# Cached grouped-query attention: the first key load cut into four transfers of interleaved partitions

## The chip, the core and the metric

The kernel runs on one core of a Trainium2 chip. The time is device time in microseconds (us) of one execution; the kernel before was timed three times. A separate execution under the hardware profiler gives the profile and the trace. The engines are named as the profile names them: PE (matrix multiply; PEld is its weight load), DVE (vector), ACT (scalar), POOL, and SP, which here only issues transfers. Transfers are carried by 16 DMA engines that work in parallel; SP and ACT each have a queue of their own that feeds them (q1 and q10 in the profile).

## The reference

Four query positions for each of 8 batches attend to a cache of 2048 keys; four query heads share one key/value head. All arrays are bf16.

```
B, Sq, D = 8, 4, 512
Hq, Hkv, Sk, Dh = 32, 8, 2048, 128
q = (x @ wq).reshape(B, Sq, Hq, Dh), heads ahead of positions
k = jnp.repeat(k_cache, rep, axis=1)
v = jnp.repeat(v_cache, rep, axis=1)
scores = jnp.einsum("bhqd,bhkd->bhqk", q, k) * (Dh ** -0.5)
p = _softmax(scores, axis=-1)
o = jnp.einsum("bhqk,bhkd->bhqd", p, v)
out = o, positions ahead of heads, reshaped (B, Sq, Hq * Dh) @ wo
```

The K cache and the V cache are 33.55 MB each, wq and wo 4.19 MB each, x and the output 32 KB each. All of it is read or written once, 75.56 MB.

## The kernel before

The work is cut into 8 passes (`NU`), numbered u = 0 to 7. A pass takes 8 pairs of a batch and a key/value head: 4 heads of batches 6 and 7 in pass 0, all 8 heads of one batch in passes 1 to 6 (`single(u)`), the other 4 heads of batches 6 and 7 in pass 7. A pass needs one K tile and one V tile of 4.19 MB each, 128 partitions by 32 KB. In passes 0 and 7 a tile has two members, one for each of the two batches, of 16 KB in a partition; a V tile has two members in every pass.

The tiles go through `ring`, a buffer with four slots (`NR`). The list `loads` fixes their order: K0, wq, K1, V0, K2, V1, K3, V2, K4, V3, K5, V4, K6, V5, K7, V6, V7, wo. `issue(done)` sends out every load whose slot is free by then: four loads ahead of the first pass, and two more after each later pass. Transfers are issued by SP, in this order, and SP waits until the slot's last reader has finished. The one exception is the second member of K0, which ACT issues, so that both members start together.

`load_kv` issues one tile. With `by_member` it makes two transfers, one for each member (line 133: 128 partitions by 16 KB, 2 MB each); with `whole` one transfer of 4 MB; with `by_half` two that each hold one half of both members. The list `split` names the loads that go by member: V0, V1, V2, V3 and K7; K0 does so by its own call. The last V goes by halves, all others go whole. wo is loaded in six pieces that get smaller to the end (line 146): 2 MB, 1 MB, 512 KB, 256 KB, 128 KB, 128 KB. Each transfer of 128 partitions has eight partitions for each of the 16 DMA engines.

Completion is told by eight counters that the transfers take in turn. A transfer waits until the one that had its counter before, eight transfers earlier, has landed.

A pass does this: DVE transposes K in eight steps (`turn(u, i, t)`, line 213; t is a quarter of the tile, and i in passes 0 and 7 is the member), in the order t = 0 with i = 0 and 1, t = 1 with i = 0 and 1, and so on. PE multiplies each turned quarter with the queries (`scores`, line 251, 32 matmuls in a pass). DVE takes the maximum (line 264), ACT the exponential (line 291), DVE transposes the weights (line 305), and copies spread them into `p_bd` (line 315). Then PE multiplies the weights of the pass before with its V tile (`values(u - 1, h)`, line 331, two halves of 32 matmuls; the right side of each matmul holds both members of V). PE's order in a pass is `scores(u)`, then the collecting of an earlier pass's output by tokens (`by_tokens`, line 375), then `values(u - 1)`. After pass 7 come `values(7, 0)`, `by_tokens(6)`, `values(7, 1)`, `project(0, 0, 4)`, `by_tokens(7)`, `project(0, 4, 16)` and `project(1, 0, 16)`. `project(gg, r0, r1)` multiplies with wo row block by row block (line 403, two matmuls for each r); r = 0 to 15 of gg = 1 are the ones that need the five small pieces of wo, cut at r = 8, 12, 14 and 15.

Ahead of pass 0, x goes through PE (line 416) and is multiplied with wq (line 425).

Of the kernel before, what the change touches and what calls it, by code (L numbers as in the profile page):

```python
# [17 lines left out]
def kernel(  # L18
# [9 lines left out]
    nc = tc.nc  # L28
# [8 lines left out]
    G = 4  # L37
    S = 128 // G
    C = Sk // S
    NG = Hkv // G  # L40
    NB = 2
    NU = B * Hkv // (G * NB)
    NS1 = NU - NG
    FIRST, LAST = 0, NU - 1
# [28 lines left out]
    ring = ring_pool.tile([128, NR, NB, C * Dh], BF16, name="ring")  # L73
# [14 lines left out]
    def single(u):  # L88
        return FIRST < u < LAST

    def half_of(u):
        return NG - 1 if u == LAST else 0
# [8 lines left out]
    def take(key):  # L101
        slot_of[key] = n_loads[0] % NR
        n_loads[0] += 1
        return slot_of[key]
# [2 lines left out]
    by_half = [(0, 0.5), (0.5, 1)]  # L107
    by_member = None

    def load_kv(kind, u, parts, engines=(nc.sync,)):  # L110

        slot = take((kind, u))
        cache = k_cache if kind == "k" else v_cache
        n = C * Dh
        if not single(u):
            rows = cache[NS1:, G * half_of(u) : G * half_of(u) + G].rearrange(
                "b g (s c) d -> (g s) b (c d)", c=C
            )
        elif kind == "v":
            rows = cache[u - 1].rearrange("(b g) (s c) d -> (g s) b (c d)", g=G, c=C)  # L120
        else:
            rows = cache[u - 1].rearrange("h (s c) d -> (h s) (c d)", c=NS * C)
        if kind == "k" and single(u):
            pairs = [(ring[:, slot, :, :].rearrange("p b n -> p (b n)"), rows)]
        elif parts is by_member:
            pairs = [(ring[:, slot, b, :], rows[:, b]) for b in range(NB)]
        else:
            pairs = [
                (ring[:, slot, :, int(h0 * n) : int(h1 * n)], rows[:, :, int(h0 * n) : int(h1 * n)])
                for h0, h1 in parts  # L130
            ]
        for i, (to, of) in enumerate(pairs):
            engines[i % len(engines)].dma_start(to, of)

    def load_wq():
        slot = take("wq")
        nc.sync.dma_start(
            ring[:, slot, :, :].rearrange("p b n -> p (b n)"), wq.rearrange("(p r) n -> p (r n)", r=R)
        )

    def load_wo():
        slot = take("wo")
        for gg, cuts in ((0, (0, RW)), (1, (0, 8, 12, 14, 15, RW))):
            rows = wo[gg * G * 512 : (gg + 1) * G * 512, :].rearrange("(p r) j -> p (r j)", r=RW)
            for r0, r1 in zip(cuts, cuts[1:]):
                nc.sync.dma_start(ring[:, slot, gg, r0 * D : r1 * D], rows[:, r0 * D : r1 * D])  # L146
# [5 lines left out]
            loads.append(("k", u + 2))  # L152
    loads.append("wo")
    loads.reverse()
    split = [("v", 0), ("v", 1), ("v", 2), ("v", 3), ("k", NU - 1)]

    def issue(done):

        while loads and n_loads[0] < done + NR:
            what = loads.pop()  # L160
            if what == "k0":
                load_kv("k", 0, by_member, (nc.sync, nc.scalar))
                nc.sync.dma_start(x_sb[:, :], x.flatten_outer_dims())
            elif what == "wq":
                load_wq()
            elif what == "wo":
                load_wo()
            elif what in split:
                load_kv(*what, by_member)
            else:  # L170
                load_kv(*what, by_half if what == ("v", NU - 1) else whole)

    issue(0)

    make_identity(nc, ident[:])
# [266 lines left out]
    for u in range(NU + 1):  # L442
# [19 lines left out]
        if u >= 1:  # L462
# [7 lines left out]
            if u == NU:  # L470
                joined(u - 1)
        issue(2 + 2 * u)

    o_last = psum_o.tile([128, DH], FP32, tag="o", name="o_last")
# [40 lines left out]
```

## Time and profile before

| what | us |
|---|---|
| median of three runs (184.38 to 184.55) | 184.46 |
| the profiled execution: its own time | 184.68 |
| the profiled execution: its span | 182.7 |
| PE busy | 135.3 (74%) |
| DVE busy | 128.5 (70%) |
| ACT busy | 70.2 (38%) |
| POOL busy | 39.1 (21%) |
| time of the packets of q1 and q10, share of 16 DMA engines | 94.2% + 2.7% |

The span is the part of the profiled execution between its first and last recorded work; 1.98 us of its own time lie outside it. The busy times of several engines add to more than the span since they work side by side. 75.70 MB in 182.7 us are 414 GB/s over the whole span, with the empty stretches at its ends counted.

### The profile page before, as it was taken

Reading aid. Unit: us, or ns where it says so; the run is one execution under the profiler, and the core shown is the slowest. Engines: PE = TensorE matmul, PEld = TensorE weight load, DVE = VectorE, ACT = ScalarE, POOL = GpSimd, SP = SyncE. Lnnn points to the kernel's source line nnn. Section 1 sums busy time; section 2 is a strip of 40 time slices with the busy share of each in tenths; the row PEclk is TensorE's granted clock in tenths of the full one; section 3 lists DMA queues with packets and bytes.
Section 4 is the critical chain, followed back from the end, with each engine's and each line's share of the span. In section 5 each row is a group of like instructions: output and inputs, shape, how many; then the busy total and the mean of one; then the engine's idle time right before and its main releaser. Section 6 shows DMA issues by size and latency. Waiting matters only on the chain.

```text
span 182.7 us, 2386 instructions
## 1 busy us (share of the span) xinstructions
PE 135.3 (74%) x924; PEld 83.0 (45%) x924; DVE 128.5 (70%) x161; ACT 70.2 (38%) x91; POOL 39.1 (21%) x110
## 2 busy tenths in 40 slices
PE   0000077922999989998999995989399977899993
PEld 0000022400358536833963682358234852388971
DVE  6518024749985997899599856995399559967340
ACT  2000020049407912970692098009900792073010
POOL 8800006008003400700160052004400220023000
PEclk9999996996599999999999999999879999999999
DMA  6999999999999998999999999999999999999991
GB/s 226 430 484 402 416 459 405 430 445 441 459 384 430 447 459 382 430 441 459 395 427 438 459 407 427 434 452 452 387 434 423 434 427 434 414 429 436 427 367 40
DMA packets 5066, 75.70 MB, mean 414 GB/s; under 512 B 512, under 2 KB 832, under 8 KB 1088
## 3 DMA queue, kind: packets, MB, share of 16 engines
q1 hardware_dynamic: 4912, 73.47, 94.2%
q10 hardware_dynamic: 144, 2.10, 2.7%
q8 instruction: 7, 0.11, 0.2%
q14 instruction: 3, 0.02, 0.0%
HBM read 75.53 MB, written 0.03 MB: 414 GB/s over the span
## 4 chain that ended last, share of the span: by engine, by line
DMA 43%; DVE 27%; PE 17%; issue 5%; ACT 3%; POOL 2%; SPq 1%; ACTq 0%; DVEq 0%; POOLq 0%
DVE kt L213 18%; DMA ring<-in_k_cache_dram 16%; DMA ring<-in_wo_dram 16%; DMA ring<-in_wq_dram 12%; PE s_ps L251 11%; DVE stat L264 4%; PE o_ps L331 4%; ACT p_sb L291 3%; PE psq L425 2%; DVE pt L305 2%; DVE stat L322 1%; POOL p_bd L315 1%; POOL q_bd L231 1%; SPq L146 1%; DVE stat L272 0%
## 5 line engine op out<-in xcount | busy, mean ns | idle before, releaser
L213 DVE STREAM_TRANSPOSE kt<-ring 128x1024 f32<-128x1024 f32 x64 | 73.9, 1208 | 15.2 <-DMA ring<-in_k_cache_dram 12.8
L251 PE MATMUL s_ps<-kt,q_bd 128*128 128x512 bf16 x256 | 68.2, 403 | 21.7 <-POOL q_bd L231 9.9
L331 PE MATMUL o_ps<-ring,p_bd 128*128 128x256 bf16 x512 | 57.2, 273 | 0.0
L251 PEld LDWEIGHTS <-q_bd 128*128 128x128 bf16 x256 | 24.9, 101 | 63.5 <-issue 27.6
L331 PEld LDWEIGHTS <-p_bd 128*128 128x128 bf16 x512 | 49.8, 98 | 6.0
L315 ACT COPY p_bd<-pt 32x1024 bf16<-32x1024 bf16 x44 | 45.8, 1040 | 1.5 <-DVE pt L305 1.1
L291 ACT ACTIVATE p_sb<-s_ps,stat 128x1024 bf16<-128x1024 f32 x16 | 17.7, 1110 | 72.6 <-DVE stat L272 72.6
L315 POOL COPY p_bd<-pt 32x1024 bf16<-32x1024 bf16 x16 | 17.0, 1062 | 106.4 <-DVE pt L305 93.7
L264 DVE TENSOR_REDUCE stat<-s_ps 128x1 f32<-128x1024 f32 x16 | 19.2, 1203 | 2.9 <-PE s_ps L251 2.8
L305 DVE STREAM_TRANSPOSE pt<-p_sb 128x512 f32<-128x512 f32 x16 | 11.4, 711 | 14.0 <-ACT p_sb L291 14.0
L231 POOL COPY q_bd<-qT 32x64 bf16<-32x64 bf16 x64 | 13.0, 229 | 20.5 <-DVE qT L436 18.8
L425 PE MATMUL psq<-ring,xT_sb 128*32 128x512 bf16 x32 | 3.4, 604 | 9.1 <-DMA ring<-in_wq_dram 9.1
L416 PE MATMUL xtp<-ident,x_sb 32*128 32x32 bf16 x4 | 0.3, 194 | 13.3 <-DMA x_sb<-in_x_dram 13.3
L436 DVE STREAM_TRANSPOSE qT<-q_sb 128x64 f32<-128x64 f32 x8 | 1.2, 213 | 8.6 <-ACT q_sb L432 8.6
L177 DVE MEMSET p_bd<- 128x2048 uint32 x3 | 5.3, 1765 | 2.0 <-PEq L499 1.2
L322 DVE TENSOR_SCALAR stat<-of_b,stat 128x2 f32<-128x2 f32 x8 | 6.3, 791 | 0.3
L416 PEld LDWEIGHTS <-x_sb 32*128 32x128 bf16 x4 | 0.2, 114 | 13.3 <-DMA x_sb<-in_x_dram 13.3
L425 PEld LDWEIGHTS <-xT_sb 128*32 128x32 bf16 x32 | 1.3, 139 | 10.6 <-issue 10.1
L432 ACT CAST q_sb<-psq 128x512 bf16<-128x512 f32 x2 | 1.2, 586 | 11.7 <-PE psq L425 11.7
L375 PEld LDWEIGHTS <-perm 128*128 128x128 bf16 x56 | 3.8, 97 | 1.9 <-issue 0.4
L403 PE MATMUL s_ps<-ring,oP 128*32 128x256 bf16 x32 | 4.4, 272 | 0.2
L419 ACT COPY xT_sb<-xtp 128x128 bf16<-128x128 bf16 x1 | 0.3, 266 | 11.2 <-PE xtp L416 11.2
(30 smaller groups left out, 45.3 us busy)
## 6 DMA issues: line engine op xcount, KB each, us to landing
ring<-in_k_cache_dram SPq DMA_DIRECT2D x6, 4096.0 KB, 24.1
ring<-in_v_cache_dram SPq DMA_DIRECT2D x10, 2048.0 KB, 25.3
ring<-in_v_cache_dram SPq DMA_DIRECT2D x3, 4096.0 KB, 30.1
ring<-in_k_cache_dram SPq DMA_DIRECT2D x3, 2048.0 KB, 27.2
ring<-in_wq_dram SPq DMA_DIRECT2D x1, 4096.0 KB, 21.0
ring<-in_k_cache_dram ACTq DMA_DIRECT2D x1, 2048.0 KB, 12.3
ring<-in_wo_dram SPq DMA_DIRECT2D x1, 2048.0 KB, 25.8
ring<-in_wo_dram SPq DMA_DIRECT2D x1, 1024.0 KB, 27.8
```

The lines of the kernel that those rows point to most:

```text
L177: nc.vector.memset(t[:, :, :, :, :], 0.0)
L213: nc.vector.transpose(out=out, in_=in_)
L231: nc.gpsimd.tensor_copy(out=qb[k * 32 : (k + 1) * 32, m, :, g, b, :].rearrange("w (j e) q -> w j e q", e=2), in_=qT[of * 32 : (of + 1) * 3 ...
L251: nc.tensor.matmul(s_ps[t // 2][:, t % 2, :], lhsT=q_bd[u % 2][:, m, 2 * j + e, :, :, :].rearrange("w g b q -> w (g b q)"), rhs=rhs, start ...
L264: nc.vector.tensor_reduce(out=stats[u][0][:, h : h + 1], in_=s_ps[h][:, :, :].rearrange("q t n -> q (t n)"), axis=AX, op=ALU.max, negate=True,
L291: nc.scalar.activation(out=out, in_=in_, func=EXP, bias=stats[u][1][:, :], scale=scale, accum_out=stats[u][2][:, h : h + 1],)
L305: nc.vector.transpose(out=pt[:, :, :, :].rearrange("s c q e -> s (c q e)").bitcast(FP32), in_=ps[u, h][:, :, :, :].rearrange("q c s e -> q ...
L315: copy(out=pb[rows, :, g, :, :], in_=pt[rows, :, :, :])
L322: nc.vector.tensor_scalar_mul(stats[u][3][:, :], of_b[:, :], stats[u][4][:, :])
L331: nc.tensor.matmul(o_pss[u][:, :, :], lhsT=pbs[u, h][:, i // 2, :, :, i % 2].rearrange("s g q -> s (g q)"), rhs=v[:, :, key_of(u, h, i // ...
L403: nc.tensor.matmul(out_ps[half], lhsT=oP[gg][:, r, :], rhs=w[:, r, half * DH : (half + 1) * DH], start=(gg == 0 and r == 0), stop=(gg == N ...
L425: nc.tensor.matmul(psq[g * T : (g + 1) * T, :], lhsT=xT_sb[:, r, :], rhs=w[:, (g * NB + gg) * rep * Dh : (g * NB + gg + 1) * rep * Dh], st ...
```

## The change

A new function `load_first` issues K0. Its second member is still one transfer from ACT, issued beside the first piece. Its first member goes from SP in four transfers of interleaved partitions: 0, 8, 16 ... (16 partitions), 1, 3, 5 ... (64), 2, 6, 10 ... (32), and 4, 12, 20 ... (16). They are 256 KB, 1 MB, 512 KB and 256 KB; each partition's row of 16 KB stays one run. Each of the 16 groups of eight neighbouring partitions has 1, 4, 2 and 1 partitions in them.

Three loads that went by member now go whole: V2, V3 and K7. That is three transfers fewer, so the number of transfers in the kernel stays 32, and from V6 on each has the counter that it had.

```diff
-    def load_kv(kind, u, parts, engines=(nc.sync,)):
+    def load_first():
+
+        slot = take(("k", FIRST))
+        rows = k_cache[NS1:, :G].rearrange("b g (s c) d -> (g s) b (c d)", c=C)
+        for i, (p, step) in enumerate(((0, 8), (1, 2), (2, 4), (4, 8))):
+            nc.sync.dma_start(ring[p::step, slot, 0, :], rows[p::step, 0])
+            if i == 0:
+                nc.scalar.dma_start(ring[:, slot, 1, :], rows[:, 1])
+
+    def load_kv(kind, u, parts):
...
-        for i, (to, of) in enumerate(pairs):
-            engines[i % len(engines)].dma_start(to, of)
+        for to, of in pairs:
+            nc.sync.dma_start(to, of)
...
-    split = [("v", 0), ("v", 1), ("v", 2), ("v", 3), ("k", NU - 1)]
+    split = [("v", 0), ("v", 1)]
...
             if what == "k0":
-                load_kv("k", 0, by_member, (nc.sync, nc.scalar))
+                load_first()
                 nc.sync.dma_start(x_sb[:, :], x.flatten_outer_dims())
```

Nothing that is computed changes, and the order of the instructions on PE, DVE, ACT and POOL is the same.

## The prediction

> **What bounds the kernel now.** I read the page first. Its lines on the DMA engines decide the rest:
>
> ```profile
> span 182.7 us, 2386 instructions
> ...
> DMA  6999999999999998999999999999999999999991
> ...
> DMA 43%; DVE 27%; PE 17%; issue 5%; ACT 3%; POOL 2%; SPq 1%; ACTq 0%; DVEq 0%; POOLq 0%
> ```
>
> The DMA engines are busy from the first slice to the last, and no engine of the core comes near that (PE 74%). The chain names DVE and PE for some stretches only because a transfer is issued when they free its slot; the row of nines says that the queue holds work all the same. So the end is the start of the stream, plus bytes over rate, plus what follows the last piece of wo. Next I looked at the start in short windows (time of each engine, then granted clock, DMA share, GB/s; a packet of 16 KB is booked where it begins, which is why a share can exceed 1):
>
> ```profile
> 1.70:1.85 0.15, 0.00 (x0) 0.00 (x0) 0.15 (x1) 0.15 (x1) 0.15 (x1) 1.00 3.40 874
> 1.85:2.40 0.55, 0.00 (x0) 0.00 (x0) 0.55 (x1) 0.55 (x1) 0.55 (x2) 1.00 0.74 238
> 2.40:2.70 0.30, 0.00 (x0) 0.00 (x0) 0.30 (x1) 0.06 (x1) 0.30 (x1) 1.00 0.00 0
> 1.74:5.74 4.00, 0.00 (x0) 0.00 (x0) 3.25 (x3) 0.72 (x1) 4.00 (x3) 1.00 1.01 385
> 100.00:170.00 70.00, 60.26 (x423) 39.57 (x421) 53.33 (x66) 31.16 (x40) 12.68 (x30) 0.98 1.00 428
> 179.40:181.20 1.80, 0.51 (x4) 0.12 (x3) 0.41 (x1) 0.36 (x1) 0.00 (x0) 1.00 0.00 0
> 181.20:181.40 0.20, 0.00 (x0) 0.00 (x0) 0.00 (x0) 0.00 (x0) 0.00 (x0) 1.00 0.42 118
> ```
>
> 874 GB/s x 0.15 us = 131 KB, eight packets; 238 x 0.55 = 131 KB, eight more; then none until 2.70. So eight of the 16 engines begin by 1.85 and the other eight straggle in over the next half microsecond. Steadily, a packet takes 16 x 16.38 KB / 428 GB/s = 0.61 us. The first eight take 3.40 x 0.15 x 16 / 8 = 1.02 us each, the second eight 0.74 x 0.55 x 16 / 8 = 0.81. From 1.74 to 5.74 the stream is (428 - 385) x 4.00 / 428 = 0.40 us short; as booking at the start flatters a window by half a packet on average (0.30), the **start loss** is about 0.7 us. The last two rows are the output's transfer of 32 partitions, used below.
>
> SP's queue (start, duration) gives the price of an issue:
>
> ```profile
> 0.75 0.37 SPq L133 DMA_DIRECT2D ring<-in_k_cache_dram  x1
> 1.17 0.42 SPq L163 DMA_DIRECT2D x_sb<-in_x_dram  x1
> 1.64 0.42 SPq L137 DMA_DIRECT2D ring<-in_wq_dram  x1
> 34.41 0.33 SPq L133 DMA_DIRECT2D ring<-in_k_cache_dram  x1
> 180.42 0.35 SPq L484 DMA_DIRECT2D out_dram<-out_sb  x1
> ```
>
> Then passes 6 and 7, where the change touches K7 (start, duration, engine, count, idle before):
>
> ```profile
> 130.87 6.88 DVE L213 STREAM_TRANSPOSE kt<-ring 128x1024 f32<-128x1024 f32 x6 [3.21 <-DMA ring<-in_k_cache_dram]
> ...
> 141.62 7.15 PE L331 MATMUL o_ps<-ring,p_bd 128*128 128x256 bf16 x64
> ...
> 147.18 1.23 DVE L213 STREAM_TRANSPOSE kt<-ring 128x1024 f32<-128x1024 f32 x1
> ...
> 150.26 5.75 DVE L213 STREAM_TRANSPOSE kt<-ring 128x1024 f32<-128x1024 f32 x5 [1.85 <-DMA ring<-in_k_cache_dram]
> ...
> 160.04 10.64 PE L331 MATMUL o_ps<-ring,p_bd 128*128 128x256 bf16 x96
> ```
>
> and the last matmuls with wo:
>
> ```profile
> 177.91 0.27 PE L403 MATMUL s_ps<-ring,oP 128*32 128x256 bf16 x1
> ...
> 178.29 0.27 PE L403 MATMUL s_ps<-ring,oP 128*32 128x256 bf16 x1
> ...
> 179.00 0.27 PE L403 MATMUL s_ps<-ring,oP 128*32 128x256 bf16 x1
> ...
> 179.34 0.27 PE L403 MATMUL s_ps<-ring,oP 128*32 128x256 bf16 x1
> ...
> 179.64 0.27 PE L403 MATMUL s_ps<-ring,oP 128*32 128x256 bf16 x1
> ```
>
> In pass 7 the first turn (147.18) is done with K7's first member alone; DVE then idles 1.85 us for the second. In the tail PE paces itself at 0.108 us per row block until r = 7 (177.91), and from there waits for each piece of wo: r = 8 at 178.29, 12 at 179.00, 14 at 179.34, 15 at 179.64.
>
> **The change, part by part.** *The start.* The first piece has one packet for each of 16 engines. Whether all 16 then begin together no row shows for 16 partitions. The nearest is the output's transfer: issued at 180.42, its first packet begins between 181.25 and 181.30 (narrower windows), 0.83 to 0.88 us later, while the 128-partition K0 needed 0.95 to 1.00 (0.75 to 1.70-1.75). So the first packet moves forward by 0 (if 0.95 belongs to a cold queue) to 0.15 us. The straggling of the second eight, 0.03 to 0.66 us behind the first, some 0.4 on average, is worth about 0.2 averaged over 16 engines and up to 0.6 on the slowest. Against it: packets that begin together may all take the 1.02 us of the first eight, not 0.81: minus 0.1. What counts is the slowest engine, since a landing is complete with its last engine. Bounds for the gain g: -0.1 (nothing is gained, eight packets take 0.2 us more) and 0.85 (all of the 0.7 goes, and 0.15 of head start). I take **g = 0.35 us**: 0.6 for the slowest engine's late begin less 0.2 to 0.4 for its longer first packet, plus 0.05 of head start. Nothing starves behind the first piece: ACT's half gives every engine eight packets (4.9 us) and the second piece is issued at 0.75 + 0.42.
>
> *More issues on SP.* Three more, at the spacing of the rows above (0.42 and 0.47), put x's issue from 1.17 to about 2.5, wq's to 3.0, K1's to 3.4, V0's to 4. K0 alone keeps the DMA engines to 1.74 + 4.19 MB / 428 GB/s = 11.5, so each of them still enters a full queue: 0. x goes to PE ahead of wq, which waits until 22.71 for its data, so x may be 9 us late for nothing. The work of four transfers in place of one: r = 14 and r = 15 wait for pieces of 128 KB that come 179.64 - 179.34 = 0.30 us apart, and 131 KB / 428 GB/s is 0.31. A further transfer in a full queue costs the stream nothing that shows; bounds 0 and 3 x 0.03, taken 0.
>
> [...]
>
> *The counters.* SP's issue of V0's second half comes to wait for ACT's half of K0, which lands at about 13 us (the first turn begins at 12.94). Until then 14.7 MB have been issued and about 4.9 moved; the 9.8 MB left cover 23 us, and the next issue, K2 at 34.41, waits for DVE anyway: 0. Without that cover it would be 9 us.
>
> *V2 and V3 whole.* Each matmul of L331 reads both members, so a first member alone starts nothing: 0. *K7 whole* takes away the early turn. Now all eight turns follow the landing, as in pass 6: from its first turn to its values matmuls 141.62 - 130.87 = 10.75 us (pass 5: 111.25 to 122.00, the same 10.75). Pass 7 then starts its values at 150.26 - g + 10.75 = 161.01 - g in place of 160.04. PE runs almost without a pause from there to r = 7, so that stretch shifts by +0.97 - g: r = 7 at 178.88 - g. The pieces of wo land g earlier, and PE meets them later: without waits r = 15 follows eight steps of 0.108 later, at 179.75 - g, against 179.64 with waits now. Of 0.97 us, 0.86 are hidden by the waits for wo and **0.11 reach the end**. Bounds: 0 (if PE closes up elsewhere) and 0.97 (if the pieces of wo moved with it).
>
> **Sum**: +0.11 - 0.35 = -0.24 us. On the profiled execution's 184.68 us that makes 184.44; the median of the runs is 0.22 lower, so on its scale **184.2 us**, 0.13% below 184.46. Under about 0.2% (0.37 us) a measurement of this kernel can't be told from no change.
>
> **The rivals.**
> 1. *The start gain is large* (g of 0.6 to 0.85): the slowest engine loses straggle and long first packet both, or PE makes up its 0.11. For it: the output's transfer starts quickly. Against: the eight that did begin together were the ones with 1.02 us. Price: 0.11 - 0.7 = -0.6, 183.85 us.
> 2. *The split gains nothing* (g = 0): the stragglers come from the queue's own first use, and ACT's simultaneous half, not from 128 partitions in one transfer. Then K7's 0.11 stands alone: 184.57 us. [...]
> 3. *Slower: PE runs at half clock in pass 7's scores.* PE is idle from 148.8 until the first turn of K7 ends, 2.4 us in place of 1.9. The windows of granted clock show a half-speed stretch behind idle times of 2.6 us (26.1 to 28.7), 3.1 (129.2 to 132.3) and over 4 (40 to 44.6), none behind 2.2 (110.4 to 112.6); it decides from somewhere between. In pass 6 one such stretch of 3.4 us was made up. In pass 1 two followed each other, and its scores ended 1.8 us after the last turn in place of 1.1: 0.7 late, with no slack left in the tail. 184.46 + 0.11 + 0.7 - 0.35 = 184.9 us; with g near 0 it is 185.3.
>
> **Chances.** Forecast 0.47 (within it 0.05 fall below the bound), rival 1 0.33, rival 2 0.08, rival 3 0.12. That makes faster 0.38, same 0.42 + 0.08 = 0.50, slower 0.12. The forecast's own range, g from 0.1 to 0.6, is 183.95 to 184.5. For 8 in 10 I go to 183.7, the far half of rival 1 (g = 0.85, to 183.72), and to 184.8, short of rival 3.
>
> **What would show it.** Right: 16 packets beginning within 0.15 us at 1.6 to 1.75, the first window without a straggle; x issued at 2.5; eight turns of K7 in one run behind its landing near 149.9, values of pass 6 near 160.7, and the last row blocks of wo at an even 0.108 us with no waits. Wrong: a second group of engines starting late again (rival 2), a granted clock of 0.5 between 150 and 160 (rival 3), waits for wo still there at the end (K7's cover was not needed), or a thin slice in the DMA row near 13 to 35 us (the counter's wait was not covered).

## The result and the profile after

The changed kernel is slower. Six runs have a median of 187.16 us (186.55 to 188.04), six of the kernel before on the same chip 184.51 us (184.38 to 184.84): a ratio of 1.0146, with a 95% interval of 1.0115 to 1.0177. The profiled execution took 187.35 us with a span of 185.5, which is 2.8 us more span than before. Some executions of such kernels are disturbed and some per cent longer (189.2 to 191.4 us for the kernel before, beside the experiments); the ratios here leave them out, and since the profiles of three experiments (act_late, both_on_sp, by_columns) are of such executions, only their first 12 us are read.

The profile page after (span, the DMA row of 40 slices, shares of the chain of waits):

```profile
span 185.5 us, 2389 instructions
...
DMA  6999999999999999999999999999999999999990
...
DMA 41%; PE 27%; DVE 20%; issue 4%; ACT 3%; POOL 2%; SPq 2%; ACTq 0%; DVEq 0%; POOLq 0%
```

The row of nines is unbroken, so the DMA engines were never without work. That does not say how much they carried. The same windows of both kernels do (start and end, width, the five engines, granted clock, DMA share, GB/s). Before:

```profile
1.74:5.74 4.00, 0.00 (x0) 0.00 (x0) 3.25 (x3) 0.72 (x1) 4.00 (x3) 1.00 1.01 385
5.74:8.74 3.00, 0.00 (x0) 0.00 (x0) 1.75 (x3) 0.00 (x0) 2.51 (x10) 1.00 1.02 437
8.74:10.74 2.00, 0.00 (x0) 0.00 (x0) 0.00 (x0) 0.00 (x0) 0.00 (x0) 1.00 1.01 434
10.74:16.74 6.00, 0.31 (x4) 0.31 (x5) 3.80 (x4) 0.27 (x1) 0.00 (x0) 1.00 1.01 434
16.74:32.74 16.00, 7.39 (x43) 2.71 (x43) 5.05 (x12) 1.17 (x2) 3.24 (x16) 0.89 1.00 431
32.74:102.74 70.00, 60.19 (x355) 33.80 (x353) 59.58 (x70) 34.84 (x43) 15.55 (x46) 0.95 1.01 432
```

After:

```profile
1.74:5.74 4.00, 0.00 (x0) 0.00 (x0) 3.25 (x3) 0.69 (x1) 4.00 (x3) 1.00 0.99 336
5.74:8.74 3.00, 0.00 (x0) 0.00 (x0) 1.75 (x3) 0.00 (x0) 2.52 (x10) 1.00 1.02 284
8.74:10.74 2.00, 0.00 (x0) 0.00 (x0) 0.00 (x0) 0.00 (x0) 0.00 (x0) 1.00 0.98 418
10.74:16.74 6.00, 0.32 (x4) 0.21 (x4) 0.51 (x1) 0.04 (x1) 0.00 (x0) 1.00 1.07 374
16.74:32.74 16.00, 4.44 (x36) 1.84 (x37) 7.61 (x14) 1.39 (x3) 2.44 (x12) 0.98 0.99 428
32.74:102.74 70.00, 60.65 (x352) 33.81 (x350) 57.40 (x68) 34.85 (x43) 16.45 (x50) 0.93 1.01 432
```

The missing bytes of a window, divided by 431 GB/s, are time. The first window lost (385 - 336) x 4.00 / 431 = 0.45 us, the second 1.06, the third 0.07, the fourth 0.84, the fifth 0.11 and the sixth nothing: 2.5 us, nearly all of the loss, and all in the time in which K0 and what was queued beside it moved. At 1.02 the engines are as busy from 5.74 to 8.74 as before, but each packet lasts longer. The mean time of a packet is the share times 16 engines times 16.38 KB over the rate: 1.02 x 262 / 284 = **0.94 us**, where before it is 1.02 x 262 / 437 = **0.61 us**.

The packets of each queue from 0 to 5 us (packets, MB, share of the 16 engines) show the other thing. Before, and then after:

```profile
q1 hardware_dynamic: 43, 0.70, 39.6%
q10 hardware_dynamic: 32, 0.52, 26.4%
```

```profile
DMA packets 64, 1.05 MB, mean 210 GB/s; under 512 B 0, under 2 KB 0, under 8 KB 0
...
q10 hardware_dynamic: 64, 1.05, 65.2%
```

Before, the two halves of K0 run side by side from the start. After, SP's queue (q1) has no packet at all in the first 5 us. Yet SP issued its pieces from 0.74 on (its timeline: start, duration, count):

```profile
0.74 2.52 SPq L115 DMA_DIRECT2D ring<-in_k_cache_dram  x4
3.31 0.58 SPq L172 DMA_DIRECT2D x_sb<-in_x_dram  x1
3.93 0.42 SPq L146 DMA_DIRECT2D ring<-in_wq_dram  x1
...
11.41 0.80 SPq L142 DMA_DIRECT2D ring<-in_v_cache_dram  x2
```

In narrow windows SP's first packet begins at 5.42 us, when ACT's queue (q10) has begun 73 of its 128. The first piece of 256 KB lands 8.2 us after its issue, at 8.9 us.

Pass 7 and the end (start, duration; the values of pass 6 are the line with L340):

```profile
152.63 6.88 DVE L222 STREAM_TRANSPOSE kt<-ring 128x1024 f32<-128x1024 f32 x6 [2.99 <-DMA ring<-in_k_cache_dram]
...
163.39 7.80 PE L340 MATMUL o_ps<-ring,p_bd 128*128 128x256 bf16 x70
...
181.81 0.27 PE L412 MATMUL s_ps<-ring,oP 128*32 128x256 bf16 x1
...
181.91 0.27 PE L412 MATMUL s_ps<-ring,oP 128*32 128x256 bf16 x1
...
182.03 0.27 PE L412 MATMUL s_ps<-ring,oP 128*32 128x256 bf16 x1
...
182.13 0.27 PE L412 MATMUL s_ps<-ring,oP 128*32 128x256 bf16 x1
```

The eight turns of K7 follow its landing in one run, and the last row blocks of wo stand an even 0.11 us apart, without waits. The first turn is 152.63 - 150.26 = 2.37 us later than before, the last matmul 182.13 - 179.64 = 2.49. So 0.12 us come from the end of the kernel and the rest was there by then.

### The profile page after: what moved, and what is told of

Read it like the earlier page. It is cut to its first block, busy times and chain, and to the rows that moved or that the text cites. A ratio compares the mean times of both kernels' runs of the same rounds, so it can differ in the third digit from the quotient of the medians.

```text
span 185.5 us, 2389 instructions
## 1 busy us (share of the span) xinstructions
PE 135.6 (73%) x924; PEld 83.2 (45%) x924; DVE 128.5 (69%) x161; ACT 70.2 (38%) x91; POOL 39.3 (21%) x110
## 4 chain that ended last, share of the span: by engine, by line
DMA 41%; PE 27%; DVE 20%; issue 4%; ACT 3%; POOL 2%; SPq 2%; ACTq 0%; DVEq 0%; POOLq 0%
DMA ring<-in_k_cache_dram 29%; PE s_ps L260 15%; DVE kt L222 14%; DMA ring<-in_wq_dram 12%; PE o_ps L340 8%; DVE stat L273 3%; ACT p_sb L300 2%; PE psq L434 2%; PE s_ps L412 2%; SPq L115 1%; DVE pt L314 1%; POOL p_bd L324 1%; DVE stat L331 1%; POOL q_bd L240 1%; POOL q_bd L237 0%
## 5 line engine op out<-in xcount | busy, mean ns | idle before, releaser
L260 PE MATMUL s_ps<-kt,q_bd 128*128 128x512 bf16 x256 | 69.2, 411 | 21.1 <-POOL q_bd L240 9.9
L340 PE MATMUL o_ps<-ring,p_bd 128*128 128x256 bf16 x512 | 57.2, 273 | 0.0
L340 PEld LDWEIGHTS <-p_bd 128*128 128x128 bf16 x512 | 49.8, 98 | 5.8
L352 ACT ACTIVATE o_sb<-o_ps,stat 128x128 bf16<-128x128 f32 x8 | 2.9, 368 | 3.9 <-PE o_ps L340 3.8
```

The source lines that it names most:

```text
L260: nc.tensor.matmul(s_ps[t // 2][:, t % 2, :], lhsT=q_bd[u % 2][:, m, 2 * j + e, :, :, :].rearrange("w g b q -> w (g b q)"), rhs=rhs, start ...
L340: nc.tensor.matmul(o_pss[u][:, :, :], lhsT=pbs[u, h][:, i // 2, :, :, i % 2].rearrange("s g q -> s (g q)"), rhs=v[:, :, key_of(u, h, i // ...
```

## The experiments

Two theories stood against each other after this. *Held back*: SP's pieces wait for part of the other queue's transfer. *Partition groups*: packets into some sets of partitions take longer than into others (0.94 us on average here, against 0.61 before). Further ones were that K7 whole costs the time, that the short pieces run dry, and that the rows read from memory matter. In the expectations *held back* is A, later F, with its rival G (a transfer with a step is slow to prepare by itself); *partition groups* is D; short pieces are B, the later loads C, the rows in memory H. Ratios are to the kernel before, run on the same chip beside the experiment, with a 95% interval. The edits are against the changed kernel except where said.

### contiguous: the same four sizes, neighbouring partitions

```diff
-        for i, (p, step) in enumerate(((0, 8), (1, 2), (2, 4), (4, 8))):
-            nc.sync.dma_start(ring[p::step, slot, 0, :], rows[p::step, 0])
+        for i, (p0, p1) in enumerate(((0, 16), (16, 80), (80, 112), (112, 128))):
+            nc.sync.dma_start(ring[p0:p1, slot, 0, :], rows[p0:p1, 0])
```

> The four transfers keep their sizes and their order, but take neighbouring partitions: 0 to 15, 16 to 79, 80 to 111, 112 to 127. Everything else is as in the changed kernel (median 187.16 us). Theory A, the step between the partitions delays SP's first packets: with neighbours q1's first packet begins near 1.75 us as before the change, the slow packets near 6 and 13 us are gone, and the time is 184.4 to 184.9 us. Theory B, the two pieces that give an engine a single packet make its queue run dry, whatever their partitions: q1's first packet stays near 5 us and the time stays at 186.5 to 188. Theory C, the loss is not in the start but in what is done with V2, V3 and K7: no change, 186.5 to 188.

Measured: 1.0400 (1.0374 to 1.0427), 191.45 us. The same bytes in the same number of transfers cost 191.45 - 187.16 = 4.3 us more than interleaved ones do. Its windows:

```profile
5.74:8.74 3.00, 0.00 (x0) 0.00 (x0) 1.75 (x3) 0.00 (x0) 2.51 (x10) 1.00 1.07 350
8.74:12.74 4.00, 0.00 (x0) 0.00 (x0) 0.00 (x0) 0.00 (x0) 0.00 (x0) 1.00 0.99 274
```

From 8.74 on a packet lasts 0.99 x 262 / 274 = 0.95 us. Which partitions a piece goes to decides, not how many pieces there are. Its first packet of SP began at 1.77 us, so its first piece was not held back, as theory A had it; but the second, of 64 neighbouring partitions, began only at 6.62, when q10 had begun 79 packets. None of the three theories had a slower kernel: A was right on the first packet and 7 us off in the time.

### evenodd: two interleaved pieces

```diff
-        for i, (p, step) in enumerate(((0, 8), (1, 2), (2, 4), (4, 8))):
+        for i, (p, step) in enumerate(((0, 2), (1, 2))):
...
-    split = [("v", 0), ("v", 1)]
+    split = [("v", 0), ("v", 1), ("v", 2), ("k", NU - 1)]
```

> K0's first member goes in two transfers, the even partitions (64) and the odd ones (64), so the step stays and no piece is short; V2 and K7 go by member as before the change, V3 whole, which keeps the number of transfers. Theory A (the step): q1's first packet is late as in the changed kernel and 1 to 2.5 us are lost, 185.5 to 187. Theory B (single packets): four packets for each engine in each piece, nothing runs dry, 184.3 to 184.7.

Measured: 1.0026 (1.0007 to 1.0044). Its packets from 0 to 5 us, and then its second window:

```profile
q10 hardware_dynamic: 64, 1.05, 66.3%
```

```profile
5.74:8.74 3.00, 0.00 (x0) 0.00 (x0) 1.75 (x3) 0.00 (x0) 2.51 (x10) 1.00 1.02 437
```

It is held back just like the changed kernel (64 packets of q10, none of q1), but has no slow packets. So the first is there without the second, and costs about 0.0026 x 184.5 = 0.48 us (0.13 to 0.81 by the interval, from two runs); the first window after had lost 0.45. That is less than theory A had (1 to 2.5 us) and a little more than B had.

### start_alone and whole_alone: the change in two parts

start_alone keeps the new first load and splits the later ones as before. whole_alone is the kernel before with only the later loads whole.

```diff
start_alone, against the changed kernel
-    split = [("v", 0), ("v", 1)]
+    split = [("v", 0), ("v", 1), ("v", 2), ("v", 3), ("k", NU - 1)]
whole_alone, against the kernel before
-    split = [("v", 0), ("v", 1), ("v", 2), ("v", 3), ("k", NU - 1)]
+    split = [("v", 0), ("v", 1)]
```

> K0 goes in the four interleaved pieces as in the changed kernel, V2, V3 and K7 by member as before it. Theories A and B (the loss is in the start): the landing of K1 stays about 3 us later than before the change, and the time is that of the changed kernel less the 0.1 us forecast for K7, 186.4 to 187.9. Theory C (the loss is in the loads that became whole): 184.2 to 184.7.

> K0 goes in two transfers as before the change, V2, V3 and K7 go whole as after it. Forecast of the prediction's tail term: pass 6's values begin 0.97 us later, of which 0.11 reach the end, 184.5 to 184.7 us; the eight turns of K7 run without a pause. Theory C: 186.5 or more.

Measured: start_alone 1.0156 (1.0140 to 1.0171), whole_alone 1.0021 (1.0002 to 1.0039). The start alone has all of the loss. The later loads add little: whole_alone is 0.33 and 0.43 us above the median of before in two runs, where 0.11 was forecast; by the interval it is 0.04 to 0.72 us, so 0.11 is neither confirmed nor refuted. Its trace:

```profile
150.06 6.88 DVE L213 STREAM_TRANSPOSE kt<-ring 128x1024 f32<-128x1024 f32 x6 [3.00 <-DMA ring<-in_k_cache_dram]
...
160.81 10.43 PE L331 MATMUL o_ps<-ring,p_bd 128*128 128x256 bf16 x94
```

The turns and then the values are 160.81 - 150.06 = 10.75 us apart, as forecast.

### quarters_step and quarters_block: four equal pieces, other partitions

Both send four pieces of 32 partitions from SP, ACT's half beside the first; they differ only in which partitions make up a piece.

```diff
quarters_step
+        for i, (p, step) in enumerate(((0, 4), (1, 4), (2, 4), (3, 4))):
             nc.sync.dma_start(ring[p::step, slot, 0, :], rows[p::step, 0])
quarters_block
+        for i, (p0, p1) in enumerate(((0, 32), (32, 64), (64, 96), (96, 128))):
+            nc.sync.dma_start(ring[p0:p1, slot, 0, :], rows[p0:p1, 0])
```

> K0's first member goes in four transfers of 32 partitions each, every fourth one: 0, 4, 8 ...; 1, 5, 9 ...; and so on; the rest as in the changed kernel. [...] Theory B, short pieces run dry: two packets for each engine in each piece, between the changed kernel's one and the four of the even and odd run, so some of the loss stays: 185.5 to 187. [...]

> The same four transfers of 32 partitions each, but of neighbours: 0 to 31, 32 to 63, 64 to 95, 96 to 127. [...] Theory B, the size of the pieces alone decides: the same time as with every fourth partition.

Measured: quarters_step 1.0039 (1.0023 to 1.0054; 185.36 us; of the 0.0039 x 184.5 = 0.72 us, evenodd's 0.48 and the 0.11 forecast for K7 make 0.59), quarters_block 1.0308 (1.0252 to 1.0365). The windows of quarters_step, then of quarters_block:

```profile
5.74:8.74 3.00, 0.00 (x0) 0.00 (x0) 1.75 (x3) 0.00 (x0) 2.50 (x10) 1.00 1.01 431
8.74:12.74 4.00, 0.00 (x0) 0.00 (x0) 0.00 (x0) 0.00 (x0) 0.00 (x0) 1.00 1.08 460
```

```profile
5.74:8.74 3.00, 0.00 (x0) 0.00 (x0) 1.74 (x3) 0.00 (x0) 2.51 (x10) 1.00 1.10 328
8.74:12.74 4.00, 0.00 (x0) 0.00 (x0) 0.00 (x0) 0.00 (x0) 0.00 (x0) 1.00 0.98 287
```

A packet takes 1.01 x 262 / 431 = 0.61 us in the first, and 1.10 x 262 / 328 = 0.88 and 0.98 x 262 / 287 = 0.89 us in the second. Size and number of the pieces are the same, so the partitions make the difference, some 5 us. And here the two mechanisms part the other way round. The packets of quarters_step from 0 to 5 us, then those of quarters_block:

```profile
q10 hardware_dynamic: 64, 1.05, 65.5%
```

```profile
q10 hardware_dynamic: 30, 0.49, 40.4%
q1 hardware_dynamic: 32, 0.52, 35.5%
```

quarters_step is held back, and its packets take 0.61 us; quarters_block starts at once beside ACT's half, and its packets take 0.88 us and more.

So a packet's time goes with the partitions that the pieces take. In means over both queues' packets it is 0.61 us with steps of 2 and 4 (evenodd, quarters_step), 0.94 in the change, which has the step of 8, and 0.88 to 0.95 with the blocks (quarters_block, and contiguous from 8.74 on); the dearest kernel, at 1.0400, is the one with the blocks of 16. By what mechanism some sets of partitions are slow, no run shows. The loss is 2.0 us in the change's windows from 5.74 to 16.74, and 0.0308 x 184.5 = 5.7 in all in quarters_block.

The trace of the changed kernel shows which packets lengthen. The packets of the first piece (q1, from 5.42 to 6.3 us), then those of ACT's transfer right behind them (q10, from 6.3 to 7.5):

```profile
q1 hardware_dynamic: 16, 0.26, 108.3%
```

```profile
q10 hardware_dynamic: 16, 0.26, 102.4%
```

A packet of the piece takes 1.083 x 16 x 0.88 / 16 = 0.95 us, and a packet of ACT's, which goes to all 128 partitions, 1.024 x 16 x 1.2 / 16 = 1.23. From 5.42 to 8.6 q10 has 39 packets (69.6% of the engines' time, 0.91 us each). Above 0.61 each that makes 39 x 0.30 / 16 = 0.73 us for ACT's packets and 16 x 0.34 / 16 = 0.34 for the piece's own, together about the 1.06 us that the second window lost. So two thirds of that loss are in the packets of the other transfer; why they lengthen, no run shows. It also speaks against one more explanation, that a piece is dealt out to a few engines only: the 16 packets all begin within 0.88 us, and as the engines have 16 packets under way at a time (a share of about 1) and one takes at least 0.61, hardly any engine can have had two of them one behind the other.

### one_queue: no transfer from ACT beside the pieces

```diff
-        for i, (p, step) in enumerate(((0, 8), (1, 2), (2, 4), (4, 8))):
+        for p, step in ((0, 8), (1, 2), (2, 4), (4, 8)):
             nc.sync.dma_start(ring[p::step, slot, 0, :], rows[p::step, 0])
-            if i == 0:
-                nc.scalar.dma_start(ring[:, slot, 1, :], rows[:, 1])
+        nc.sync.dma_start(ring[:, slot, 1, :], rows[:, 1])
```

> The four interleaved pieces as in the changed kernel, but K0's second member is issued by SP behind them, none by ACT. Theory F, SP's first piece comes late because it stands behind ACT's transfer: its packets begin at 1.6 to 1.8 us. Theory G, a transfer with a step between its partitions takes some 4 us to be prepared, whatever stands beside it: its packets begin near 5 us, the DMA engines stay empty until then, and the time is 189 to 191. By F the slow packets of the two pieces of 16 partitions stay and the second piece may leave a gap: 186 to 188.

Measured: 1.0097 (1.0064 to 1.0131).

```profile
1.70:2.05 0.35, 0.00 (x0) 0.00 (x0) 0.35 (x1) 0.32 (x1) 0.35 (x1) 1.00 0.00 0
2.05:2.20 0.15, 0.00 (x0) 0.00 (x0) 0.15 (x1) 0.00 (x0) 0.15 (x2) 1.00 2.99 874
...
5.74:8.74 3.00, 0.00 (x0) 0.00 (x0) 1.75 (x3) 0.00 (x0) 2.51 (x10) 1.00 1.08 355
```

Without ACT's transfer the first piece begins at 2.1 us and not at 5.4: it was ACT's transfer that it stood behind. Theory G is out. Part of the loss probably goes with ACT's transfer (two runs, and the interval overlaps a little with that of the change, 1.0115 to 1.0177). The rest stays, with packets of 1.08 x 262 / 355 = 0.80 us in the third of these windows. This run answers a question of the prediction too: with nothing beside it, the first interleaved piece begins 0.37 us later than the first half of K0 did before (2.11 against 1.74).

### sources_block: interleaved partitions, rows of memory in blocks

The pieces go to the partitions of the change; the rows that they read are neighbouring blocks (so the keys of four heads of batch 6 stand in another order).

```diff
-        for i, (p, step) in enumerate(((0, 8), (1, 2), (2, 4), (4, 8))):
-            nc.sync.dma_start(ring[p::step, slot, 0, :], rows[p::step, 0])
+        for i, (p, step, r0, r1) in enumerate(((0, 8, 0, 16), (1, 2, 16, 80), (2, 4, 80, 112), (4, 8, 112, 128))):
+            nc.sync.dma_start(ring[p::step, slot, 0, :], rows[r0:r1, 0])
```

> The destinations as in the changed kernel, but each piece reads a block of neighbouring rows of K (0 to 15, 16 to 79, 80 to 111, 112 to 127), so K0's first member stands in the buffer in another order and the output of batch 6's first four heads is another. Theory D (destinations): the slow packets of the pieces of 16 partitions stay, 186.5 to 188. Theory H, the sources are what is slow, because 16 engines read rows 128 KB apart: slow packets gone, 184.8 to 185.3.

Measured: 1.0155 (1.0090 to 1.0221), with a packet of 1.03 x 262 / 333 = 0.81 us in the second window:

```profile
5.74:8.74 3.00, 0.00 (x0) 0.00 (x0) 1.75 (x3) 0.00 (x0) 2.51 (x10) 1.00 1.03 333
```

The loss is that of the changed kernel. So the rows in memory do not make it; the partitions of SBUF do. (The packet is 0.81 us here against 0.94; a small share of the rows in that is not excluded.)

### both_on_sp: what the second queue was worth before

Against the kernel before; both halves of K0 go from SP.

```diff
-                load_kv("k", 0, by_member, (nc.sync, nc.scalar))
+                load_kv("k", 0, by_member)
```

> The kernel before, but both members of K0 go from SP, one behind the other, each as one transfer of 128 partitions; ACT issues none. With no second queue beside the first packets: if ACT's simultaneous transfer takes something from the start of the kernel before, the start loss of 0.7 us shrinks and the time is 184.1 to 184.4; if not, it is the 184.5 of the kernel before. A loss is possible only by the 0.4 us that every further issue on SP moves x and wq back, which the queue covers.

Measured: 1.0027 (1.0016 to 1.0038). Starting both halves at once is worth about 0.5 us, where the expectation had a gain or nothing. That is as much as evenodd lost, whose halves start one behind the other as well. The first packets show how. From 1.7 to 3.0 us before, then after:

```profile
q1 hardware_dynamic: 16, 0.26, 70.6%
q10 hardware_dynamic: 13, 0.21, 45.3%
```

```profile
q10 hardware_dynamic: 21, 0.34, 124.0%
```

Before, a packet takes (0.706 + 0.453) x 16 x 1.3 / 29 = 0.83 us; after, with one transfer alone in flight, 1.240 x 16 x 1.3 / 21 = 1.23. In the same stretch both_on_sp has 21 packets at 120.0%, 1.19 us each, though it has no interleaved piece at all, and evenodd 20 at 123.5%, 1.28. So standing back does not leave the engines empty (the share from 1.74 to 5.74 is 0.99): what it costs is in the longer first packets of the transfer that starts alone.

### act_late and pieces_on_act: who stands back

act_late has the pieces of quarters_step and puts a small copy on ACT ahead of ACT's issue. The trace has that issue at 0.98 us, 0.24 behind SP's first and not the 2 us of the expectation; the copy itself runs at 2.04. pieces_on_act changes the roles: the four interleaved pieces of the change go from ACT, the other half from SP in one transfer.

```diff
act_late
-        for i, (p, step) in enumerate(((0, 8), (1, 2), (2, 4), (4, 8))):
+        late = const.tile([128, 64], FP32, name="late")
+        nc.vector.memset(late[:, :], 0.0)
+        nc.scalar.copy(out=late[:, :32], in_=late[:, 32:])
+        for p, step in ((0, 4), (1, 4), (2, 4), (3, 4)):
             nc.sync.dma_start(ring[p::step, slot, 0, :], rows[p::step, 0])
-            if i == 0:
-                nc.scalar.dma_start(ring[:, slot, 1, :], rows[:, 1])
+        nc.scalar.dma_start(ring[:, slot, 1, :], rows[:, 1])
pieces_on_act
-        for i, (p, step) in enumerate(((0, 8), (1, 2), (2, 4), (4, 8))):
-            nc.sync.dma_start(ring[p::step, slot, 0, :], rows[p::step, 0])
-            if i == 0:
-                nc.scalar.dma_start(ring[:, slot, 1, :], rows[:, 1])
+        nc.sync.dma_start(ring[:, slot, 1, :], rows[:, 1])
+        for p, step in ((0, 8), (1, 2), (2, 4), (4, 8)):
+            nc.scalar.dma_start(ring[p::step, slot, 0, :], rows[p::step, 0])
```

> The four pieces of every fourth partition as in quarters_step, but ACT issues K0's second member behind a small copy, about 2 us later, when SP has issued its first pieces. Theory F in the form that the transfer issued first holds the other queue back: SP's first packets begin near 2.1 us as with one queue, and ACT's come later. In the form that any transfer of ACT in flight holds back a transfer with a step: SP's first packets are again several us late. Time 184.9 to 185.5 by both, the first packets tell them apart.

> The four pieces of the changed kernel go from ACT, the second member whole from SP, both queues from the same moment. If a transfer with a step stands back behind a whole one whichever queue it is in, ACT's first packets begin only near 5 us and SP's at 1.75; if SP's queue was the one at a disadvantage, ACT's pieces begin by 2.2. The two pieces of 16 partitions give slow packets in both cases; time 186 to 188.

Measured: pieces_on_act 1.0187 (1.0148 to 1.0225, two runs). act_late has no ratio: its only two runs took 191.99 and 196.14 us, far outside the expected 184.9 to 185.5, and whether the edit itself costs anything stays open. The packets from 0 to 5 us of act_late, then of pieces_on_act:

```profile
q1 hardware_dynamic: 37, 0.52, 40.2%
q10 hardware_dynamic: 24, 0.39, 18.4%
```

```profile
q1 hardware_dynamic: 65, 1.06, 66.5%
```

With the roles changed it is SP's whole transfer that goes first and ACT's pieces that stand back, until 5.27 us. So it is not one queue that comes before the other: issued at the same moment, the interleaved pieces stand back behind the whole transfer. In act_late, where SP's first piece is issued 0.24 us ahead, it is the other way round. The piece begins at 2.08 us, and the whole transfer stands back: its first packet comes at 3.64, when the piece has begun 31 of its 32. The packets up to 3.64 us:

```profile
q1 hardware_dynamic: 31, 0.51, 53.7%
```

By 5 us no data packet of the second piece has begun (37 packets of q1, but the 0.52 MB of the first piece's 32 alone). So which transfer was issued first, or was ready first, decides here too: the first form of theory F, that the one issued first holds the other queue back, fits this run, and the second form does not.

### by_columns: short pieces of all 128 partitions

```diff
-        for i, (p, step) in enumerate(((0, 8), (1, 2), (2, 4), (4, 8))):
-            nc.sync.dma_start(ring[p::step, slot, 0, :], rows[p::step, 0])
+        n = C * Dh // 8
+        for i, (c0, c1) in enumerate(((0, 1), (1, 5), (5, 7), (7, 8))):
+            nc.sync.dma_start(ring[:, slot, 0, c0 * n : c1 * n], rows[:, 0, c0 * n : c1 * n])
...
-    split = [("v", 0), ("v", 1)]
+    split = [("v", 0), ("v", 1), ("k", NU - 1)]
```

> The four pieces keep their bytes (256 KB, 1 MB, 512 KB, 256 KB) but each takes all 128 partitions and an eighth, a half, a quarter and an eighth of the 16 KB of a partition; K7 goes by member again. [...] Theory D (partition groups): no slow packets near 6 and 13 us, and as the pieces have no step, SP's first packets begin at 1.75: 184.2 to 184.8, that of the kernel before; below it if the small first packets shorten the start loss. Theory B (a short piece runs its queue dry, whatever its partitions): slow packets or gaps behind the first and the last piece, 185.5 to 187.

Measured: 1.0026 (1.0012 to 1.0040), 0.48 us, just above the range of theory D and below that of B. The pieces have the sizes of the change (256 KB, 1 MB, 512 KB, 256 KB) but reach all partitions:

```profile
5.74:8.74 3.00, 0.00 (x0) 0.00 (x0) 1.75 (x3) 0.00 (x0) 2.51 (x10) 1.00 0.95 384
```

384 GB/s against 284 for the change in this window. Short pieces alone do not make the 2 us, since the whole loss here is 0.48. They gain nothing either: no kernel tried was faster than the kernel before.

## Why the prediction was wrong

It forecast 184.2 us (183.7 to 184.8) and chances of 0.38, 0.50 and 0.12. It is 187.16.

- **What bounds the kernel** was right: the end is the start of the stream, plus bytes over rate, plus the tail, and a loss at the start came out at the end nearly whole (2.37 us at K7's first turn, 2.49 at the last matmul).
- **The start, g = 0.35 us, is the step that failed**, in sign and size: about -2.4 us, far outside its bounds of -0.1 and 0.85. Both bounds took the four pieces to carry bytes as one transfer of 128 partitions does, and the nearest row was taken from the output's transfer of 32 partitions only for its first packet, not for its rate. Two sentences of that step fell. "Nothing starves behind the first piece" took the two queues to share the engines as before; instead q1 had no packet in 5 us while q10 had 64. The engines were not empty, but the first packets took 1.23 us in place of 0.83, so the start loss grew where it was to shrink: 0.45 us in the first window, 0.48 in evenodd. And the packets of the pieces of 16 partitions were taken at the steady 0.61 us, or at worst the 1.02 of a first packet, once; instead the first piece's took 0.95 us, ACT's behind them 1.23, and the mean of all packets was 0.94 us for 3 us; the rate fell again from 10.74 to 16.74, the stretch in which the last piece of 16 partitions was due: 2.0 us together. quarters_step against quarters_block shows that the partitions do this (0.61 us against 0.88); by what mechanism, no run shows.
- **The head start** of 0 to 0.15 us was not there: the interleaved first piece begins at 2.11 us even alone (one_queue), 0.37 later than before.
- **More issues on SP** cost nothing that shows at the end, though each took 0.57 to 0.61 us in place of the 0.37 forecast from; x was issued at 3.31, not 2.5. The queue stayed full.
- **The counters** cost nothing: SP's issue of V0 waited until 11.41, ahead of the 13 us forecast, and K1 and wq covered it (428 GB/s from 16.74 to 32.74, where before had 431).
- **The tail** was right: 10.76 us from first turn to values (10.75 forecast), no waits for wo at the end, 0.12 us through to the last matmul (0.11 forecast).
- **The rivals.** The second (the split gains nothing, 184.57) had the sign, but no cost for the split. The third's mechanism did occur, with half clock (0.51) in pass 7's scores, but the stretch from first turn to values was 10.76 us all the same, so it cost nothing there, though its 184.9 to 185.3 came nearest by the number:

```profile
155.00:158.40 3.40, 3.39 (x10) 1.12 (x9) 3.40 (x5) 0.00 (x0) 0.00 (x0) 0.51 1.02 439
```

A rival with slower packets was missing. The cost of an operation with no row in the trace (transfers of every second, fourth and eighth partition) should have been bounded from its rate as well as from its first packet.

## What to carry to other kernels

A transfer's price depended here on which partitions it reaches, not only on its bytes: four pieces of 32 partitions cost a ratio of 1.0039 with a step of 4 and 1.0308 as blocks. Before a load is cut by partitions, measure what a packet takes in each of the pieces, and leave the load whole if it is longer than before (the cut along the columns avoided most of the loss, and gained nothing either). A busy share near 1 does not say that the stream runs at its rate (1.02 stood beside 437 GB/s before and 284 after); put the GB/s of the same windows side by side, and compute the time of a packet. When two queues are to share the engines, look at the packets of each queue in the first few microseconds, since one of them can stand back (q1 had none in 5 us here, q10 64).

## What the runs showed that was not expected

- Interleaved pieces stood back behind a whole transfer of the other queue until 70 to 73 of its 128 packets had begun: the first packet came at 5.42 us (the change) and 5.27 us (pieces_on_act), against 2.11 with no such transfer beside them. Pieces of 32 neighbouring partitions did not stand back, but contiguous's second piece, of 64, did, and in act_late the whole transfer stood back behind a piece. So the step between the partitions is not the whole reason; what decides the turns was not settled.
- The 16 packets of a 256 KB piece went along with slower packets of the other queue: 1.23 us each for ACT's, longer than the piece's own 0.95. In the second window that was some 0.73 us of the 1.06 lost, an estimate from 39 packets of 0.91 us.
- Issuing an interleaved piece keeps SP busy for longer (ns: least, median, most; first and last start in us), where a transfer of 128 partitions had taken 0.37 us. The step is not the whole reason: the neighbouring pieces of contiguous took 383/620/711.

```profile
L115 SPq DMA_DIRECT2D ring<-in_k_cache_dram x4: 570/592/613, 0.7 to 2.7; - x4
```

- Sets of 16 partitions other than every eighth and neighbouring ones were not tried, nor the interleaved pieces behind the whole half on the same queue; so the price of the step of 8 rests on the change itself and on the runs that keep its pieces.
